# Guarded turns on a shared port in a planner, and a shorter float64 conversion: attention, experts and a feed-forward layer on one core

## The chip, the cores and the metric

The kernel runs on one core of one Trainium2 chip. The metric is the device time of one execution in microseconds (us); lower is better. The engines are TensorE (PE; its weight loads are PEld), VectorE (DVE), ScalarE (ACT), GpSimd (POOL) and SyncE (SP, which issues all DMAs here).

## The reference, cut to what matters

Three layers follow each other. Windowed attention over 4 x 576 tokens with 8 heads gives x of 2304 x 512. A mixture of eight dense experts follows, whose gate P is normalized eight times over rows and columns. The last layer is

```python
h = x @ w_in
g = np.maximum(0.01 * h, h)
return (g @ w_out).astype(np.float32)
```

with w_in of 512 x 2048 and w_out of 2048 x 512. These two arrive as **float64**, because they were scaled by a float64 factor; all else is float32. The kernel sees each float64 as two 32-bit words and makes a float32 of it on the chip, once, before the last layer needs it.

## The kernel before

**Matrix work.** Every weight and activation is split into two float16 parts, and each product is a sum of three float16 matmuls. On top of that, each pair of blocks goes through a seven-product scheme (`PRODUCTS`) in place of eight. A chunk is 512 columns of one expert (16 chunks) or of the last layer (4). For each chunk and each of five token pairs p, `a_steps` makes the hidden block and `b_steps` multiplies it back and adds it to the result `acc`. Each has groups of seven steps j, six matmuls to a step for 256 columns. L1089 is the matmul of an a step, L1205 of a b step.

**What the other engines do for a step.** ScalarE and VectorE empty PSUM: ScalarE copies products to `q` (L1101, L1113), VectorE adds into a held bank (L1105), and the outer, middle and sum blocks are split into float16 parts (`h<-...` at L1117, L1136, L1142, L1158). GpSimd subtracts the high part of the sums (`sums_lo`, L1161, 128x1024), which the b steps of the same block read. The product of a b step is added to `acc` by VectorE (L1218), or, for steps 1 and 3, by ScalarE and GpSimd (L1215, L1216). For the next chunk's weights, GpSimd forms sums (L964) and low parts (L804).

**The float64 pieces.** `to_single(n, place)` converts one piece of 128x512 float64 numbers in a staging buffer `raw` (two of them, raw_173 and raw_174 in the order below). There are 32 pieces, about three to a chunk, in chunks 1 to 11. Each has a load and these jobs: `exponent` (VectorE L1018 takes the exponent bits, ScalarE L1021 shifts and rebiases them), `signed` (VectorE L1024 adds the sign bit), `high` (VectorE L1029 masks the upper mantissa, ScalarE L1030 makes 1 + x of it), `low` (ScalarE L1036 scales the lower word, GpSimd L1038 adds it), `put` (GpSimd L1042 multiplies mantissa and exponent, SP stores the piece). L1018, L1024 and L1029 read and write SBUF alone.

**The planner.** The program is written out once, and then `Plan` orders it. It makes a node of each instruction (for TensorE, of each run of matmuls into one bank) with an estimated cost. `deadlines` walks back from TensorE's ideal sequence and gives each node a latest end. `order` plays the program forward, event by event: on each engine it picks, of the nodes that are ready, the one with the earliest latest end. `fix` pins the resulting order on every engine, without waits of its own. VectorE nodes with no PSUM operand are marked `shared`: in the plan they can't start while a GpSimd instruction runs, and a GpSimd instruction that meets one of them is stretched. On the chip nothing but the order within each engine, and the data, enforces any of that: which of the two gets the port depends on who comes first there.

**An engine's queue is in order.** An instruction that waits holds up all that stands behind it on its engine. This is why the place of the piece's instructions among the others matters.

Of the kernel before, what the change touches and what calls it, by code (L numbers as in the profile page):

```python
# [30 lines left out]
class Plan:  # L31
# [15 lines left out]
    NEAR = 60.0  # L47

# [194 lines left out]
    def deadlines(self, products):  # L243
# [5 lines left out]
        for i in products:  # L249
            t += nodes[i]["cost"] + self.TURN.get((mode, nodes[i]["mode"]), 0)  # L250
            mode = nodes[i]["mode"]
            ends[i] = t
        latest = [ends.get(i, t + 5000) for i in range(n)]
# [21 lines left out]
    def order(self, latest):  # L275
# [12 lines left out]
        gpsimd, port, mode = (0.0, 0.0), (0.0, 0.0), "full"  # L288
        self.starts = [0.0] * n

# [11 lines left out]
        def takes(i, t):  # L302

            node = nodes[i]
            cost = node["cost"]
            if node["eng"] == "PE":
                cost += self.TURN.get((mode, node["mode"]), 0)
            elif node["shared"] and gpsimd[0] <= t < gpsimd[1]:
                cost = max(cost, gpsimd[1] - t + cost - node["shared"])
            elif node["eng"] == "Pool" and port[0] <= t < port[1]:  # L310
                cost += max(0.0, port[1] - t - 140)
            return cost

        for _ in range(n):
            choices = []
            for e, w in waiting.items():
                when = [(x, i) for x, i in ((since(i), i) for i in w) if x is not None]
                if when:
                    choices.append((max(free[e], min(when)[0]), e, when))
            t, eng, when = min(choices)  # L320
            at = dict((i, x) for x, i in when)
# [4 lines left out]
            if eng != "PE" and eng != "SP":  # L326

                for i in sorted((i for i in at if i != pick and at[i] < start + cost), key=lambda i: latest[i]):
                    s = max(at[i], t)
                    c = takes(i, s)  # L330
                    if (latest[i] < latest[pick] and max(at[i], start + cost) + nodes[i]["cost"] > latest[i]
                            and s + c + nodes[pick]["cost"] <= latest[pick]):
                        pick, start, cost = i, s, c
                        break
                if nodes[pick]["shared"] and cost > nodes[pick]["cost"] + 100:
                    other = [i for i in at if i != pick and not nodes[i]["shared"] and at[i] <= start + 100
                             and max(t, at[i]) + nodes[i]["cost"] + cost <= max(latest[pick], start + cost + 200)]
# [6 lines left out]
            if eng == "PE":  # L344
                mode = node["mode"]
            elif node["shared"]:
                port = (max(start, gpsimd[1]) if gpsimd[0] <= start < gpsimd[1] else start), end
            elif eng == "Pool":
                gpsimd = start, end
            self.starts[pick] = start  # L350
# [17 lines left out]

    def fix(self):
        follows = mybir.DependencyInfo(mybir.DependencyClass.NoSync, mybir.DependencyReason.DATA)  # L370
        products = [i for i, node in enumerate(self.nodes) if node["eng"] == "PE"]
        for picks in self.order(self.deadlines(products)).values():
            line = [ins for i in picks for ins in self.nodes[i]["ins"]]
            for a, b in zip(line, line[1:]):
                self.tc.add_manual_dep(b, a.name, follows, reason="order")


@with_exitstack
def attn_moe_kernel(
# [65 lines left out]
    nc.vector.memset(shift, float(-(896 << 23)))  # L445
# [550 lines left out]
    def to_single(n, place):  # L996
# [20 lines left out]
        def exponent():  # L1017
            nc.vector.tensor_scalar(out=d["fac"], in0=d["hi"], scalar1=20, scalar2=0x7FF,  # L1018
                                    op0=ALU.logical_shift_right, op1=ALU.bitwise_and)

            nc.scalar.activation(out=d["fac"], in_=d["fac"], func=AF.Relu, scale=float(2**23), bias=shift)  # L1021

# [4 lines left out]
        def high():  # L1027

            nc.vector.tensor_scalar(out=d["man"], in0=d["hi"], scalar1=0xFFFFF, scalar2=None, op0=ALU.bitwise_and)  # L1029
            nc.scalar.activation(out=d["man"].bitcast(F32), in_=d["man"], func=AF.Relu, scale=2.0**-20,  # L1030
                                 bias=ones[:, 0:1])

        def low():

            rest = d["rest"] = words_f32(d["lo"])
            nc.scalar.activation(out=rest, in_=d["lo"].bitcast(U32), func=AF.Copy, scale=2.0**-52)  # L1036
            man = d["man"].bitcast(F32)
            nc.gpsimd.tensor_tensor(out=man, in0=man, in1=rest, op=ALU.add)  # L1038
# [6 lines left out]
        def words_f32(w):  # L1045
            return w.bitcast(F32)

        return load, [exponent, signed, high, low, put]


# [443 lines left out]
```

## Time and profile before

| | |
|---|---|
| median of 3 runs | 1856.25 us (1854.02 to 1857.41) |
| the profiled execution | 1853.38 us, span of the trace 1851.6 us |
| TensorE granted clock, mean | 0.996 |
| TensorE busy | 1812.1 us |
| VectorE, ScalarE, GpSimd busy | 1367.5, 1348.8, 1323.0 us |
| DMA | 97.81 MB, mean 53 GB/s |

The attention stage takes about the first 200 us of the trace; after that the chunks follow each other, some 83.5 us each. Busy time counts an instruction from its start to its end, so an instruction that is held at a port counts as busy. Idle time of an engine that doesn't bound the kernel costs nothing.

### The profile page before, as it was taken

How to read it: one execution, taken by the hardware profiler on the slowest of the kernel's cores; microseconds unless marked ns; L12 is line 12 of the kernel's file. 1: busy time of each engine (PE TensorE's matmuls, PEld its weight loads, DVE VectorE, ACT ScalarE, POOL GpSimd, SP SyncE). 2: the span in 40 equal slices, each digit the busy share in tenths (PEclk: the TensorE clock that was granted, in tenths of full speed). 3: DMA queues.
4: the chain of work that ended last, by engine and by line, in shares of the span. 5: the costliest groups of instructions: out<-in, count | busy, mean ns of one | idle time of the engine just before them, and what ended most of it. 6: DMA issues, size and time to landing. Idle time of an engine off the chain costs nothing.

```text
span 1851.6 us, 45040 instructions
## 1 busy us (share of the span) xinstructions
PE 1812.1 (98%) x17542; PEld 1603.7 (87%) x17542; DVE 1367.5 (74%) x3656; ACT 1348.8 (73%) x3099; POOL 1323.0 (71%) x1154
## 2 busy tenths in 40 slices
PE   8899999999999999999999999999999999999999
PEld 6677888889888888889888888889898888989888
DVE  7878677777777687777777776666676888687877
ACT  8988778767767766767767667666666789877664
POOL 3943878787869788787868777676667696776753
PEclk9999999999999999999999999999999999999999
DMA  8332020311112121202111110100000000101002
GB/s 296 109 115 76 4 81 28 87 37 62 53 47 67 32 74 37 86 27 72 53 47 53 47 52 30 47 24 24 24 24 34 15 24 24 47 1 47 1 33 72
DMA packets 61096, 97.81 MB, mean 53 GB/s; under 512 B 4561, under 2 KB 27601, under 8 KB 60881
## 3 DMA queue, kind: packets, MB, share of 16 engines
q1 hardware_dynamic: 60880, 94.93, 15.6%
q8 instruction: 137, 2.24, 0.5%
q14 instruction: 79, 0.64, 0.1%
HBM read 81.81 MB, written 13.11 MB: 51 GB/s over the span
## 4 chain that ended last, share of the span: by engine, by line
PE 76%; POOL 7%; ACT 6%; DVE 5%; DMA 4%; issue 2%; SPq 0%; POOLq 0%; DVEq 0%; ACTq 0%
PE t L1205 36%; PE s L1089 20%; PE sq L1089 15%; POOL w L804 3%; DMA raw<-in_moe_w_dram 3%; POOL h L1161 1%; PE s L570 1%; PE o L669 1%; PE pt L651 1%; ACT junk L937 1%; POOL xp L804 1%; DVE s L1117 1%; DVE raw L1018 1%; ACT raw L940 1%; DVE acc L1218 1%
## 5 line engine op out<-in xcount | busy, mean ns | idle before, releaser
L1205 PE MATMUL t<-w,h 128*128 128x256 f16 x7560 | 953.3, 273 | 7.5 <-ACT acc L1212 2.7
L1089 PEld LDWEIGHTS <-w 128*128 128x128 f16 x8400 | 757.0, 98 | 101.5 <-issue 22.9
L1205 PEld LDWEIGHTS <-h 128*128 128x128 f16 x7560 | 736.1, 98 | 97.1 <-issue 8.8
L1089 PE MATMUL s<-xp,w 128*128 128x256 f16 (+1 forms) x4872 | 591.3, 262 | 13.4 <-ACT q L1101 10.2
L1218 DVE SCALAR_TENSOR_TENSOR acc<-t,pu,acc 128x256 f32<-128x256 f32 x866 | 407.3, 479 | 173.5 <-PE t L1205 149.9
L1161 POOL TENSOR_TENSOR h<-s,h 128x1024 f16<-128x1024 f32 x180 | 386.2, 2145 | 135.1 <-ACT h L1158 95.4
L1089 PE MATMUL sq<-xp,w 128*128 128x256 f16 (+1 forms) x3528 | 429.9, 262 | 1.8 <-ACT q L1101 1.0
L1216 POOL TENSOR_TENSOR acc<-acc,part 128x256 f32<-128x256 f32 x322 | 238.9, 743 | 201.0 <-ACT part L1215 131.5
L804 POOL TENSOR_TENSOR w<-raw,w 128x512 f16<-128x512 f32 x240 | 274.7, 1162 | 28.8 <-ACT w L803 28.3
L1101 ACT ACTIVATE q<-s 128x256 f32<-128x256 f32 x364 | 138.6, 381 | 134.9 <-PE s L1089 132.3
L1158 ACT ACTIVATE h<-s 128x1024 f16<-128x1024 f32 x180 | 190.1, 1056 | 45.8 <-DVE s L1117 44.4
L1117 DVE SCALAR_TENSOR_TENSOR h<-sq,h 128x512 f16<-128x512 f32 x352 | 193.1, 553 | 34.0 <-ACT h L1136 24.4
L1215 ACT ACTIVATE part<-t,pu 128x256 f32<-128x256 f32 x322 | 152.1, 472 | 79.8 <-PE t L1205 75.0
L1105 DVE SCALAR_TENSOR_TENSOR sq<-s,q 128x256 f32<-128x256 f32 x176 | 75.8, 431 | 143.5 <-PE s L1089 86.3
L1105 DVE SCALAR_TENSOR_TENSOR sq<-sq,q 128x256 f32<-128x256 f32 x352 | 150.3, 427 | 38.1 <-PE sq L1089 33.6
L803 ACT ACTIVATE w<-raw 128x512 f16<-128x512 f32 x240 | 147.5, 631 | 12.1 <-PE s L1089 4.3
L1117 DVE SCALAR_TENSOR_TENSOR s<-sq,s 128x256 f32<-128x256 f32 x352 | 146.4, 416 | 0.7
L1136 ACT ACTIVATE h<-sq 128x512 f16<-128x512 f32 x176 | 104.9, 596 | 55.6 <-DVE sq L1105 46.5
L1117 DVE SCALAR_TENSOR_TENSOR s<-sq,q 128x256 f32<-128x256 f32 x352 | 137.1, 417 | 9.4 <-ACT q L1113 7.8
L940 ACT ACTIVATE raw<-raw,sr 128x512 f32<-128x512 f32 x160 | 109.7, 720 | 7.4 <-DVE sr L795 7.4
L937 ACT ACTIVATE junk<-raw 128x512 bf16<-128x512 f32 x160 | 100.4, 627 | 14.6 <-DMA raw<-in_moe_w_dram 9.1
L964 POOL TENSOR_TENSOR raw<-raw 128x512 f32<-128x512 f32 x80 | 102.4, 1280 | 0.0
(151 smaller groups left out, 1682.9 us busy)
## 6 DMA issues: line engine op xcount, KB each, us to landing
raw<-in_moe_w_dram SPq DMA_DIRECT2D x32, 768.0 KB, 4.7
k_t<-in_k_dram SPq DMA_DIRECT2D x16, 512.0 KB, 4.6
raw<-in_moe_w_dram SPq DMA_DIRECT2D x32, 256.0 KB, 3.6
raw<-in_moe_w_in_dram SPq DMA_DIRECT2D x16, 512.0 KB, 3.5
raw<-in_moe_w_out_dram SPq DMA_DIRECT2D x16, 512.0 KB, 3.5
q_t<-in_q_dram SPq DMA_DIRECT2D x18, 256.0 KB, 2.9
acc<-in_v_dram SPq DMA_DIRECT2D x18, 256.0 KB, 6.1
v_t<-in_v_dram SPq DMA_DIRECT2D x18, 256.0 KB, 2.7
```

The source lines that it names most:

```text
L803: nc.scalar.activation(out=hi, in_=src, func=AF.Copy)
L804: return nc.gpsimd.tensor_tensor(out=lo, in0=src, in1=hi, op=ALU.subtract)
L1089: nc.tensor.matmul(d[b][:, f, :], t[:, wp, kk, ft * P:(ft + 1) * P], XP[p][:, o, kk, xp, :], start=(i == 0 and f == 0 and j in FIRST), sto ...
L1101: nc.scalar.activation(out=q[:, k], in_=ps, func=AF.Copy, scale=CS)
L1105: nc.vector.scalar_tensor_tensor(out=block(k), in0=ps, scalar=CS, in1=q[:, k], op0=ALU.mult, op1=ALU.add)
L1117: nc.vector.scalar_tensor_tensor(out=out, in0=in0, scalar=sc, in1=in1, op0=op0, op1=op)
L1158: nc.scalar.activation(out=h[:, 3:7, 0, :], in_=d["s"], func=AF.Copy)
L1161: nc.gpsimd.tensor_tensor(out=h[:, 3:7, 1, :], in0=d["s"], in1=h[:, 3:7, 0, :], op=ALU.subtract)
L1205: nc.tensor.matmul(ps, h[:, o, hp, f, tt * P:(tt + 1) * P], w[:, wp, ft, :], start=(i == 0 and j in FIRST), stop=(i == 5), skip_group_chec ...
L1215: nc.scalar.activation(out=part, in_=ps, func=AF.Copy, scale=s)
L1216: nc.gpsimd.tensor_tensor(out=dst, in0=dst, in1=part, op=ALU.add)
L1218: nc.vector.scalar_tensor_tensor(out=dst, in0=ps, scalar=s, in1=dst, op0=ALU.mult, op1=ALU.add)
```

## The change

**In the planner.** (1) A GpSimd instruction that follows a shared VectorE instruction in the plan (`holder`) starts there only after it, and where its start falls within GUARD = 1500 ns of the holder's, the pair goes into `turns`; `fix` then gives the GpSimd instruction a real wait (a synchronizing dependency) on that VectorE instruction. The changed program has 120 such turns: 54 of them wait for a piece's VectorE instructions, most others for `dg` at line 780. (2) `claim` lets a shared VectorE instruction of over 230 ns that would start within REACH = 400 ns go ahead of the next GpSimd instruction, if neither becomes late by it. (3) A shared VectorE instruction that would meet a running GpSimd instruction is put behind its end, if its deadline allows, so that VectorE takes other work in between. (4) `lag`, the lateness of TensorE's plan so far, is added to the deadlines in those tests.

**In the pieces.** The mask gets a second bit operation that sets bit 20, so `man` holds 2^20 + the upper 20 mantissa bits as an integer. One VectorE instruction then adds the lower word times 2^-32 and writes float32. The exponent's bias is lowered by 20 to match. ScalarE's two instructions (L1030, L1036) and GpSimd's addition (L1038) go. The ScalarE job of `exponent` becomes a job of its own (`power`). Per piece, VectorE has four instructions instead of three, ScalarE one instead of three, GpSimd one instead of two. Line numbers of the changed kernel: L1018 becomes L1057, L1021 L1062, L1029 L1066, L1024 L1070, the new addition is L1075, L1042 L1080, L1161 L1196, L1216 L1251, L1218 L1253, L964 L1003, L804 L843, L1105 L1140, L1117 L1152.

```diff
+    REACH = 400.0
+    GUARD = 1500.0
...
             elif node["shared"] and gpsimd[0] <= t < gpsimd[1]:
                 cost = max(cost, gpsimd[1] - t + cost - node["shared"])
-            elif node["eng"] == "Pool" and port[0] <= t < port[1]:
-                cost += max(0.0, port[1] - t - 140)
...
+                if e == "DVE" and gpsimd[1] > free[e]:
+                    when = [(max(x, gpsimd[1]) if nodes[i]["shared"] and gpsimd[0] <= max(x, free[e]) < gpsimd[1]
+                             and latest[i] + lag > gpsimd[1] + nodes[i]["cost"] else x, i) for x, i in when]
...
+            if eng == "Pool":
+                if holder is not None:
+                    t = max(t, port[1] + self.TO["Pool"])
+                first = min((i for _, i in when if since(i) <= t + self.NEAR), key=lambda i: (latest[i], i), default=None)
+                wanted = self.claim(choices, latest, lag, free["DVE"], t, first)
+                if wanted is not None:
+                    eng, when = "DVE", [wanted]
+                    t = max(free["DVE"], wanted[0])
...
             if eng == "PE":
                 mode = node["mode"]
+                lag = max(lag, end - self.ends[pick])
             elif node["shared"]:
                 port = (max(start, gpsimd[1]) if gpsimd[0] <= start < gpsimd[1] else start), end
+                holder = pick
             elif eng == "Pool":
                 gpsimd = start, end
+                if holder is not None and start < port[0] + self.GUARD:
+                    self.turns.append((pick, holder))
+                holder = None
...
+    def claim(self, choices, latest, lag, free, t, first):
+
+        for _, e, when in choices:
+            if e == "DVE":
+                for x, i in sorted(when, key=lambda w: latest[w[1]]):
+                    a = self.nodes[i]
+                    start = max(free, x)
+                    if a["shared"] and a["cost"] > 230 and start <= t + self.REACH:
+                        late = start + a["cost"]
+                        if any(k != i and max(y, late) + self.nodes[k]["cost"] > latest[k] + lag and latest[k] < latest[i]
+                               and y <= late for y, k in when):
+                            return None
+                        if first is not None and latest[first] < latest[i] and late + self.nodes[first]["cost"] > latest[first] + lag:
+                            return None
+                        return x, i
+        return None
...
+        after = mybir.DependencyInfo(mybir.DependencyClass.Sync, mybir.DependencyReason.DATA)
+        for i, k in self.turns:
+            self.tc.add_manual_dep(self.nodes[i]["ins"][0], self.nodes[k]["ins"][-1].name, after, reason="port")
...
-    nc.vector.memset(shift, float(-(896 << 23)))
+    nc.vector.memset(shift, float(-(916 << 23)))
...
+        def mantissa():
+
+            nc.vector.tensor_scalar(out=d["man"], in0=d["hi"], scalar1=0xFFFFF, scalar2=0x100000,
+                                    op0=ALU.bitwise_and, op1=ALU.bitwise_or)
...
-        def high():
-
-            nc.vector.tensor_scalar(out=d["man"], in0=d["hi"], scalar1=0xFFFFF, scalar2=None, op0=ALU.bitwise_and)
-            nc.scalar.activation(out=d["man"].bitcast(F32), in_=d["man"], func=AF.Relu, scale=2.0**-20,
-                                 bias=ones[:, 0:1])
-
         def low():
 
-            rest = d["rest"] = words_f32(d["lo"])
-            nc.scalar.activation(out=rest, in_=d["lo"].bitcast(U32), func=AF.Copy, scale=2.0**-52)
-            man = d["man"].bitcast(F32)
-            nc.gpsimd.tensor_tensor(out=man, in0=man, in1=rest, op=ALU.add)
+            nc.vector.scalar_tensor_tensor(out=d["man"].bitcast(F32), in0=d["lo"].bitcast(U32), scalar=2.0**-32,
+                                           in1=d["man"], op0=ALU.mult, op1=ALU.add)
...
-        return load, [exponent, signed, high, low, put]
+        return load, [exponent, power, mantissa, signed, low, put]
```

**VectorE at the 28th piece** (raw_173, the first of its chunk; in the trace of before its L1018 starts at 989.63 us). sq, s and h are the PSUM banks and blocks of an a step, acc the result of a b step. Before:

```order
L1117 SCALAR_TENSOR_TENSOR s<-sq,s 128x256
L1218 SCALAR_TENSOR_TENSOR acc_107<-t_15228,pu,acc_107 128x256
L1218 SCALAR_TENSOR_TENSOR acc_109<-t_15172,pu,acc_109 128x256
L1218 SCALAR_TENSOR_TENSOR acc_110<-t_15275,pu,acc_110 128x256
L1018 TENSOR_SCALAR raw_173<-raw_173 128x512
L1105 SCALAR_TENSOR_TENSOR sq<-sq,q 128x256
L1218 SCALAR_TENSOR_TENSOR acc_109<-t_15172,pu,acc_109 128x256
L1024 SCALAR_TENSOR_TENSOR raw_173<-raw_173,sign 128x512
L1029 TENSOR_SCALAR raw_173<-raw_173 128x512
L1105 SCALAR_TENSOR_TENSOR sq<-s_15267,q 128x256
```

And now:

```order
L1152 SCALAR_TENSOR_TENSOR h<-sq,h 128x256
L1057 TENSOR_SCALAR raw_173<-raw_173 128x512
L1066 TENSOR_SCALAR raw_173<-raw_173 128x512
L1152 SCALAR_TENSOR_TENSOR s<-sq,q 128x256
L1253 SCALAR_TENSOR_TENSOR acc_109<-t_15118,pu,acc_109 128x256
L1152 SCALAR_TENSOR_TENSOR s<-sq,q 128x256
L1152 SCALAR_TENSOR_TENSOR s<-sq,s 128x256
L1253 SCALAR_TENSOR_TENSOR acc_107<-t_15174,pu,acc_107 128x256
L1152 SCALAR_TENSOR_TENSOR s<-sq,s 128x256
L1253 SCALAR_TENSOR_TENSOR acc_110<-t_15221,pu,acc_110 128x256
L1070 SCALAR_TENSOR_TENSOR raw_173<-raw_173,sign 128x512
L1075 SCALAR_TENSOR_TENSOR raw_173<-raw_173 128x512
```

The piece's instructions moved ahead of the four s sums and stand in two pairs, the exponent with the mask, and the sign with the new addition.

**GpSimd at the same place.** h is the low part of an a block's sums, w the low part of a weight. Before:

```order
L804 TENSOR_TENSOR w_15187<-raw_173,w_15187 128x512
L1216 TENSOR_TENSOR acc_107<-acc_107,part 128x256
L964 TENSOR_TENSOR t_15044<-raw_174 128x512
L1161 TENSOR_TENSOR h<-s,h 128x4x256
L964 TENSOR_TENSOR raw_174<-raw_174,t_15044 128x2x256
L1216 TENSOR_TENSOR acc_110<-acc_110,part 128x256
```

And now, with the engines that each instruction waits for (a number behind a name is the semaphore's own):

```order
L1251 TENSOR_TENSOR acc_107<-acc_107,part 128x256 [waits DVE_49]
L843 TENSOR_TENSOR w_15133<-raw_173,w_15133 128x512 [waits Activation_49]
L1196 TENSOR_TENSOR h<-s,h 128x4x256 [waits DVE_49]
L1196 TENSOR_TENSOR h<-s,h 128x4x256 [waits DVE_49,Activation_49]
L1003 TENSOR_TENSOR raw_174<-raw_174 128x2x256 [waits Pool_49]
L1251 TENSOR_TENSOR acc_110<-acc_110,part 128x256 [waits Activation_49]
```

Two h subtractions now stand in a row behind the w's; the first waits for L1066 (the mask), the second for L1075 (the addition). Before, six instructions stood between the two.

**GpSimd in the attention stage**, near 80 us of the trace. Before:

```order
L804 TENSOR_TENSOR w_732<-raw_174,w_732 128x512
L804 TENSOR_TENSOR w_735<-raw_174,w_735 128x512
L618 TENSOR_TENSOR pieces<-pieces 128x8 x2
L1161 TENSOR_TENSOR h<-s,h 128x4x256
L804 TENSOR_TENSOR w_738<-raw_174,w_738 128x512
L804 TENSOR_TENSOR w_741<-raw_174,w_741 128x512
L1161 TENSOR_TENSOR h<-s,h 128x4x256
L538 MEMSET dist 64x192
```

And now:

```order
L657 TENSOR_TENSOR pieces<-pieces 128x8 x2
L843 TENSOR_TENSOR w_729<-t_681,w_729 128x512
L1196 TENSOR_TENSOR h<-s,h 128x4x256 x2
L843 TENSOR_TENSOR w_732<-raw_174,w_732 128x512
L843 TENSOR_TENSOR w_735<-raw_174,w_735 128x512
L843 TENSOR_TENSOR w_738<-raw_174,w_738 128x512
L843 TENSOR_TENSOR w_741<-raw_174,w_741 128x512
L894 TENSOR_TENSOR sx<-acc_104 128x256
```

Both h subtractions moved ahead of four w's.

## Rows read from the trace of the kernel before

**Rows 1.** part 1 of the page: busy us, share, instructions by engine.
```profile
PE 1812.1 (98%) x17542; PEld 1603.7 (87%) x17542; DVE 1367.5 (74%) x3656; ACT 1348.8 (73%) x3099; POOL 1323.0 (71%) x1154
```

**Rows 2.** TensorE's waits, 900 to 1100 us: waiter <- releaser: total us, times, longest.
```profile
PE s L1089 <- ACT q L1101: 7.0, 3, 2.6
PE s L1089 <- DVE k L792: 0.5, 1, 0.5
```

**Rows 3.** TensorE's waits, 250 to 900 us, two of three.
```profile
PE s L1089 <- DVE sq L1105: 1.7, 6, 0.7
PE t L1205 <- DVE acc L1218: 0.7, 2, 0.5
```

**Rows 4.** TensorE's waits, 0 to 250 us, three of 17.
```profile
PE s L1089 <- ACT q L1101: 2.6, 2, 1.4
PE t L1205 <- ACT acc L1212: 1.8, 1, 1.8
PE t L1205 <- POOL h L1161: 1.6, 1, 1.6
```

**Rows 5.** timeline of the second stall: start us, us, engine, line, op, [idle before <-releaser].
```profile
989.63 3.97 DVE L1018 TENSOR_SCALAR raw<-raw 128x512 int32<-128x512 int32 x1
993.52 0.42 DVE L1105 SCALAR_TENSOR_TENSOR sq<-sq,q 128x256 f32<-128x256 f32 x1
...
988.73 1.28 POOL L964 TENSOR_TENSOR t<-raw 128x512 f32<-128x512 f32 x1
989.96 2.14 POOL L1161 TENSOR_TENSOR h<-s,h 128x1024 f16<-128x1024 f32 x1
992.05 1.27 POOL L964 TENSOR_TENSOR raw<-raw,t 128x512 f32<-128x512 f32 x1
...
993.63 0.72 ACT L1021 ACTIVATE raw<-raw,shift 128x512 int32<-128x512 int32 x1 [4.04 <-DVE raw L1018]
994.26 0.36 ACT L1101 ACTIVATE q<-s 128x256 f32<-128x256 f32 x1
...
994.68 0.82 PE L1089 MATMUL s<-xp,w 128*128 128x256 f16 x6 [2.21 <-ACT q L1101]
995.33 1.18 PE L1089 MATMUL sq<-xp,w 128*128 128x256 f16 x6
...
999.62 0.82 PE L1089 MATMUL s<-xp,w 128*128 128x256 f16 x6
```

**Rows 6.** groups by line and shape, whole run: xcount | busy us, mean ns | idle.
```profile
L1018 DVE TENSOR_SCALAR raw<-raw 128x512 int32<-128x512 int32 x32 | 31.8, 995 | 4.0 <-DMA raw<-in_moe_w_in_dram 2.4 <-DMA raw<-in_moe_w_out_dram 1.3
L1029 DVE TENSOR_SCALAR raw<-raw 128x512 int32<-128x512 int32 x32 | 23.4, 730 | 0.0
L1030 ACT ACTIVATE raw<-raw,ones 128x512 f32<-128x512 int32 x32 | 23.0, 719 | 14.7 <-DVE raw L1029 14.7
L1036 ACT ACTIVATE raw<-raw 128x512 f32<-128x512 uint32 x32 | 21.6, 675 | 0.0
L1038 POOL TENSOR_TENSOR raw<-raw 128x512 f32<-128x512 f32 x32 | 41.3, 1290 | 36.9 <-ACT raw L1036 17.6 <-DVE acc L1218 7.4 <-issue 5.7
```

**Rows 7.** instructions of a line: durations ns min/median/max, first and last start.
```profile
L1024 DVE SCALAR_TENSOR_TENSOR raw<-raw,sign x32: 741/752/1750, 236.5 to 1101.9; 128x512 int32<-128x512 int32 x32
L1018 DVE TENSOR_SCALAR raw<-raw x32: 414/650/4328, 234.1 to 1100.7; 128x512 int32<-128x512 int32 x32
```

**Rows 8.** two stretches: length, busy us (count) of each engine, granted clock, DMA.
```profile
84.20:91.20 7.00, 5.44 (x29) 3.69 (x28) 5.13 (x8) 4.81 (x16) 4.94 (x6) 0.51 0.47 152
995.60:999.10 3.50, 3.50 (x20) 2.51 (x18) 1.88 (x4) 1.87 (x4) 2.35 (x3) 0.51 0.00 0
```

**Rows 9.** timeline of a wait in the attention stage, columns as in group 5.
```profile
82.96 4.53 DVE L1117 SCALAR_TENSOR_TENSOR h<-q,h 128x768 f16<-128x768 f32 x2
...
83.84 2.83 POOL L1161 TENSOR_TENSOR h<-s,h 128x1024 f16<-128x1024 f32 x1
...
86.73 2.96 PE L1205 MATMUL t<-w,h 128*128 128x256 f16 x13 [1.56 <-POOL h L1161]
```

More of the change, by code (lines that the diff above doesn't have):

```diff
@@ L252, in deadlines @@
             ends[i] = t
+        self.ends = ends
         latest = [ends.get(i, t + 5000) for i in range(n)]
@@ L287, in order @@
         closed = dict.fromkeys(self.users, 0.0)
-        gpsimd, port, mode = (0.0, 0.0), (0.0, 0.0), "full"
+        gpsimd, port, mode, holder = (0.0, 0.0), (0.0, 0.0), "full", None
         self.starts = [0.0] * n
+        self.turns = []
+        lag = 0.0
         def since(i):
@@ L330, in order @@
                     c = takes(i, s)
-                    if (latest[i] < latest[pick] and max(at[i], start + cost) + nodes[i]["cost"] > latest[i]
-                            and s + c + nodes[pick]["cost"] <= latest[pick]):
+                    if (latest[i] < latest[pick] and max(at[i], start + cost) + nodes[i]["cost"] > latest[i] + lag
+                            and s + c + nodes[pick]["cost"] <= latest[pick] + lag):
                         pick, start, cost = i, s, c
@@ L336, in order @@
                     other = [i for i in at if i != pick and not nodes[i]["shared"] and at[i] <= start + 100
-                             and max(t, at[i]) + nodes[i]["cost"] + cost <= max(latest[pick], start + cost + 200)]
+                             and max(t, at[i]) + nodes[i]["cost"] + cost <= max(latest[pick] + lag, start + cost + 200)]
                     if other:
@@ L1019, in exponent, with power @@
                                     op0=ALU.logical_shift_right, op1=ALU.bitwise_and)
+        def power():
             nc.scalar.activation(out=d["fac"], in_=d["fac"], func=AF.Relu, scale=float(2**23), bias=shift)
+        def mantissa():
+            nc.vector.tensor_scalar(out=d["man"], in0=d["hi"], scalar1=0xFFFFF, scalar2=0x100000,
+                                    op0=ALU.bitwise_and, op1=ALU.bitwise_or)
         def signed():
@@ L1043, in put @@
             nc.sync.dma_start(dst, man)
-        def words_f32(w):
-            return w.bitcast(F32)
-        return load, [exponent, signed, high, low, put]
+        return load, [exponent, power, mantissa, signed, low, put]
     Ht = {}
```

## The prediction

> **What bounds the kernel now.** I read the page's busy times first: TensorE is busy 1812.1 of 1851.6 us, VectorE, ScalarE and GpSimd 71 to 74% [rows 1]. So work that is taken off those three is worth nothing in itself; only TensorE's idle time, some 39 us, and stretches at half its clock can be won. Next I read TensorE's waits by stage. From 900 to 1100 us there are three equal ones, 7.0 us together, on ScalarE's copy q [rows 2]. From 250 to 900 us the listed waits come to little, 1.7 us in six on VectorE's sq and 0.7 us in two on acc [rows 3]. Before 250 us, in the attention stage, they are many and of many kinds; three are shown [rows 4].
>
> The timeline of the second stall names the cause [rows 5]. VectorE's exponent instruction L1018 starts at 989.63 and lasts 3.97 us, though L1018 takes 0.41 us at its shortest [rows 7]. In that time GpSimd runs three instructions back to back, 988.73 to 993.32 us, two of which began after L1018 had. L1018 ends 0.28 us behind the third. ScalarE's L1021 waits 4.04 us for it, and L1101, whose copy TensorE needs, stands behind L1021 in ScalarE's queue. TensorE loses 2.21 us. Then its granted clock falls to 0.51, the 1.2 GHz level, from about 995.6 on [rows 8]. From 995.33 to 999.62 us it does four groups of six matmuls in 4.29 us [rows 5]; at full speed a group starts 0.65 us behind the last (994.68 to 995.33), so the four cost 1.67 us more.
>
> The Trainium skill, page "SBUF — State Buffer", section "Who interferes with whom", says of the port pair that VectorE and GpSimd share that whichever "starts first gets the pair for the whole instruction; the other fully blocks". The trace agrees that one blocks the other, but not on who gets it next: by the rule L1018 would have gone when L964 ended at 990.01, and would have been done by 990.43; it ended at 993.60. By the rule no such stall exists for a guard to remove; by the row each costs about 2.3 us.
>
> **The change part by part**, against the profiled execution of 1853.38 us.
>
> *Guard and order at the three stalls.* The three are the first pieces of their chunks. In the new order the GpSimd subtraction that could overtake L1057 (the old L1018) waits for L1066 behind it, so at most one GpSimd instruction, already running, is still ahead of the pair. By the order excerpt that is a w of a weight or a shorter sum into acc. Chunks that didn't stall in this way still lost about 0.2 us once each (the six waits of 1.7 us, less the longest of 0.7, leave five of 0.2 [rows 3]). I take 7.0 down to 0.6: **-6.4 us**; bounds 0 (if the wait is only moved) and -7.0.
>
> *The clock behind the second stall.* It fell only there, after a 2.21 us stop; with no stop I take back the 1.67: **-1.7**; bounds 0 and -1.7.
>
> *Blocked VectorE work, 250 to 900 us.* L1018 averages 0.995 us and L1029, of the same shape, 0.730, against 0.414 for the shortest L1018; L1024 takes up to 1.75 against a median of 0.75 [rows 6, 7]. The waits there sum to 2.4 us [rows 3]; I take a third: **-0.8**; bounds 0 and -2.4.
>
> *What the pieces lose and gain in work.* ScalarE loses 32 x 0.719 + 32 x 0.675 = 44.6 us, GpSimd 32 x 1.290 = 41.3 us [rows 6]. Both lie beside TensorE, which had no wait on any of the three lines: **0**. Were that cover gone, they would be a gain only. VectorE gains L1075. No row shows it; the nearest is L1024, also two SBUF inputs of 512, 0.75 us at the median; bounds 0.41 (one input, L1018) and 1.75 (L1024 when held). So 32 x 0.75 = 24.0 us is added. The old three came to at least 0.995 + 0.75 + 0.730 = 2.48 us a piece (L1024 at its median); four that aren't held are 2 x 0.41 + 2 x 0.75 = 2.32. VectorE's sum thus hardly changes, and its 26% idle time hides it: **0**. If it weren't hidden, a pair of 1.5 us in the queue ahead of L1140 (the old L1105) would stop ScalarE and TensorE as L1018 did; that is the third rival.
>
> *The guards' own cost.* The 120 waits hold GpSimd, and behind it its queue: acc sums, sums and low parts of weights, the h subtractions. GpSimd has 29% idle, so most are hidden; h is the one that TensorE reads soon. A late h has cost TensorE 1.56 us once [rows 9]. No row shows a guard; bounds 0 and nine times 1.56 = 14, since nine chunks have an h behind each of the two pairs. I take half a microsecond in total for GpSimd's smaller delays, and 0.3 for shifts of order in the late chunks: **+0.8**.
>
> *The attention stage.* At 82.96 us VectorE's two h subtractions take 4.53 us, held by GpSimd; GpSimd's h, itself held (2.83 us against 2.14 at 989.96 [rows 5]), ends at 86.67, and TensorE has waited 1.56 for it [rows 9]. The clock is then at 0.51 over 84.2 to 91.2 us [rows 8]. The new order puts both GpSimd h ahead of four w's, which should end this wait; but in this stage one engine's relief is soon another's wait (2.6 us on q, 1.8 on acc [rows 4], neither at the port), and the whole order of the stage is made anew. I take the 1.56 alone: **-1.5**; bounds -8.7 (the wait; half of TensorE's 5.44 busy us in the slow stretch, 2.7; and the 2.6 and 1.8 of the other waits) and +4.3 (another wait like it, with its slow stretch).
>
> Sum: -6.4 - 1.7 - 0.8 + 0.8 - 1.5 = **-9.6 us**, so 1843.8 for an execution like the profiled one. That one was 2.87 us below the median of 1856.25, against which runs are compared; I give the time on that footing: 1856.25 - 9.6 = 1846.65, rounded to **1846.5 us**.
>
> **The rivals.**
>
> *The first of each pair still waits its turn (13%).* The guard acts on the GpSimd instruction after the pair, not on the one before. If the one ahead is an h, L1057 waits up to 2.14 us, and pair and wait take 2.14 + 2 x 0.41 = 2.96 instead of 3.97. Each stall shrinks by 1.0 us only, -3.0, and with the -0.8 of the blocked work it comes to about 1852.5. For it: VectorE has no guard against GpSimd. Against: the order excerpt has no h directly ahead.
>
> *The page's rule decides (2%).* If a held VectorE instruction always went next, the three stalls would have another cause and the guards would only make GpSimd wait: the -6.4 and -1.7 go, the time is 1856.25 - 1.5 = 1854.8. The page is the Trainium skill's "SBUF — State Buffer", cited above. Rows 5 speak against it.
>
> *The guard makes h late (10%, the slower side).* The second h of a pair waits for L1075, which stands in VectorE's queue behind sums into acc that wait for TensorE. TensorE then waits for GpSimd for VectorE for TensorE. At 1.56 us in nine chunks that is +14.0, and with the sum above 1856.25 - 9.6 + 14.0 = 1860.7. It decides from 9.6 / 9 = 1.07 us in each chunk. For it: the excerpt shows both h's in a row, later in GpSimd's queue than before. Against: over the whole run TensorE waited for an h only once [rows 4].
>
> *The attention stage falls into place (15%).* If the wait at 85 us and the low clock behind it both go, and the 1.8 on acc too, the stage gives 1.56 + 2.7 + 1.8 = 6.1 instead of 1.5: about 1842. For it: VectorE held by GpSimd stands at the root of the first two. Against: q and acc wait for ScalarE, which the change relieves only after this stage.
>
> That the guard doesn't exist as a wait is excluded: the order excerpt shows the semaphore of VectorE on both h.
>
> **How the numbers follow.** The forecast has 60%, and its own range from the bounds of the clock, the small waits and the attention stage is about 1841 to 1852. The rivals have 13, 2, 10 and 15%. A measurement here tells some 0.2%, 3.7 us, from no change: below 1852.5 is faster, above 1860 slower. Faster: nearly all of 60 (58), 15, and half of 13 (6): 79%. Slower: 6 of the 10 of the late h, whose price is just above the bound, and 2 for an attention stage that got worse: 8%. Same: the rest, 13%. Eight times in 10 it lies between 1839 and 1856: the low end is the lucky attention stage with the small waits gone, the high end the rule of the page and a little more.
>
> **What would show it.** The longest L1057 is below 2.6 us instead of 4.33; TensorE's waits between 900 and 1100 us come to about 1 us instead of 7.5, with full clock there; L1030, L1036 and L1038 have no successor, and busy time falls by about 45 us on ScalarE and 41 on GpSimd, with the span only 10 us shorter. The forecast is wrong if TensorE's waits name L1196 (the late h), if L1057 still shows 4 us, or if the first 250 us lose or win more than 5.

## The result, and the profile after

The changed kernel took **1837.85 us** in the median of 4 runs (1836.86 to 1843.13), the kernel before 1856.83 in the same comparison (1854.02 to 1868.97). The ratio is 0.9891 with an interval of 0.9844 to 0.9939: 1.1% faster, about twice the 9.6 us forecast, and 1.15 us below the range. The profiled execution of after took 1843.13 us (span 1841.3), the slowest of its four. A second profile of the same kernel (1839.62 us, span 1837.9, experiment 5) is read beside it.

Part 1 of the page, as [rows 1]:

```profile
PE 1808.0 (98%) x17542; PEld 1603.2 (87%) x17542; DVE 1331.9 (72%) x3688; ACT 1317.1 (72%) x3035; POOL 1267.4 (69%) x1122
```

VectorE has 32 instructions more and yet is busy for 35.6 us less, where the prediction had it hardly changed; ScalarE fell by 31.7 us and GpSimd by 55.6, where it had about 45 and 41. TensorE's waits from 900 to 1100 us [rows 2] are gone: the view lists none there, nor anywhere from 860 to 1130 us. From 250 to 860 us, where [rows 3] were (waiter <- releaser: total us, times, longest):

```profile
PE t L1240 <- DVE acc L1253: 2.0, 6, 0.6
PE sq L1124 <- ACT q L1136: 1.9, 2, 1.6
PE s L1124 <- DVE k L828: 0.9, 2, 0.5
PE t L1240 <- ACT part L1250: 0.6, 1, 0.6
```

And from 0 to 250 us, as [rows 4]. The 1.6 us on an h has become 0.3; the acc is later than before (2.9 us against 1.8), and the 2.6 us on rb lies at 17 us, ahead of any piece:

```profile
PE pt L690 <- ACT rb L680: 3.3, 2, 2.6
PE t L1240 <- ACT acc L1247: 2.9, 1, 2.9
...
PE s L1124 <- ACT q L1136: 1.6, 2, 1.2
...
PE rt L664 <- POOL h L1196: 0.3, 1, 0.3
```

The timeline of the 28th piece, whose L1018 stood for 3.97 us in [rows 5] (start us, us, engine, line, op, [idle before <- releaser]):

```profile
984.13 0.42 DVE L1057 TENSOR_SCALAR raw<-raw 128x512 int32<-128x512 int32 x1
...
984.46 0.42 DVE L1066 TENSOR_SCALAR raw<-raw 128x512 int32<-128x512 int32 x1
984.58 0.72 ACT L1062 ACTIVATE raw<-raw,shift 128x512 int32<-128x512 int32 x1 [0.59 <-DVE raw L1057]
...
984.96 2.13 POOL L1196 TENSOR_TENSOR h<-s,h 128x1024 f16<-128x1024 f32 x1 [0.91 <-DVE raw L1066]
...
985.57 0.38 ACT L1136 ACTIVATE q<-s 128x256 f32<-128x256 f32 x1 [0.27 <-PE s L1124]
...
987.30 0.74 DVE L1070 SCALAR_TENSOR_TENSOR raw<-raw,sign 128x512 int32<-128x512 int32 x1
...
987.96 0.69 DVE L1075 SCALAR_TENSOR_TENSOR raw<-raw 128x512 f32<-128x512 uint32 x1
...
988.79 2.13 POOL L1196 TENSOR_TENSOR h<-s,h 128x1024 f16<-128x1024 f32 x1 [1.70 <-DVE raw L1075]
```

Now GpSimd waits and VectorE does not. The first h stands 0.91 us for L1066, the second 1.70 us for L1075, and ScalarE gets to q (L1136) at once. No VectorE instruction of a piece is held by more than 0.4 us any more, at this place or elsewhere; the instructions of a line (durations ns min/median/max), as [rows 7]:

```profile
L1057 DVE TENSOR_SCALAR raw<-raw x32: 415/426/616, 233.7 to 1091.2; 128x512 int32<-128x512 int32 x32
L1066 DVE TENSOR_SCALAR raw<-raw x32: 415/420/424, 234.2 to 1091.6; 128x512 int32<-128x512 int32 x32
L1070 DVE SCALAR_TENSOR_TENSOR raw<-raw,sign x32: 740/743/1135, 235.2 to 1092.6; 128x512 int32<-128x512 int32 x32
L1075 DVE SCALAR_TENSOR_TENSOR raw<-raw x32: 678/684/689, 235.9 to 1093.3; 128x512 f32<-128x512 uint32 x32
```

GpSimd pays, as its groups show (count | busy us, mean ns | idle before, with the releasers):

```profile
L1196 POOL TENSOR_TENSOR h<-s,h 128x1024 f16<-128x1024 f32 x180 | 383.9, 2133 | 151.2 <-ACT h L1193 73.6 <-DVE acc L1253 21.7 <-DVE raw L1075 15.1
L1251 POOL TENSOR_TENSOR acc<-acc,part 128x256 f32<-128x256 f32 x322 | 232.9, 729 | 175.1 <-ACT part L1250 62.7 <-DVE raw L1075 28.6 <-DVE dg L819 19.5
L1080 POOL TENSOR_TENSOR raw<-raw 128x512 f32<-128x512 f32 x32 | 40.8, 1275 | 55.3 <-DVE raw L1075 54.1 <-DVE k L828 1.2
```

Some 98 us of waits on L1075 lie in GpSimd's idle time. Of these, 54 us stand before L1080, which multiplies what L1075 wrote and would wait for it without a guard. The guards account for the other 44 us, for 27 us on L1066 and for some 20 on dg. The listed waits of TensorE name GpSimd for 0.3 us in all. In the attention stage, the place of [rows 9] now reads:

```profile
85.28 2.14 POOL L1196 TENSOR_TENSOR h<-s,h 128x1024 f16<-128x1024 f32 x1 [0.42 <-DVE s L1152]
...
87.43 0.22 PE L664 MATMUL rt<-identb,pieces 128*112 128x128 bf16 x1 [0.29 <-POOL h L1196]
...
87.49 0.71 PE L1240 MATMUL t<-w,h 128*128 128x256 f16 x5
```

The h is no longer held (2.14 us against 2.83) and TensorE passes it with 0.29 us lost. The clock, as [rows 8] (window: length, busy us (count) of PE, PEld, DVE, ACT, POOL, granted clock, DMA):

```profile
20.90:27.90 7.00, 6.39 (x41) 4.65 (x39) 3.61 (x18) 5.72 (x21) 0.00 (x0) 0.51 0.85 295
84.20:91.20 7.00, 6.61 (x102) 5.34 (x100) 6.49 (x16) 6.67 (x18) 5.62 (x4) 1.00 0.14 40
184.70:188.30 3.60, 3.32 (x17) 2.32 (x17) 0.92 (x2) 2.51 (x7) 3.60 (x4) 0.53 0.00 0
975.00:1000.00 25.00, 25.00 (x232) 22.41 (x229) 17.36 (x42) 16.76 (x35) 22.39 (x20) 1.00 0.06 22
```

The stretches of before at 84 and 996 us are at 2.4 GHz now. One at 185 us is still there, as before (186.6 to 190.2 us at 0.53), and one at 21 us, which before's profiled execution did not have. In the second profile of after neither is there; its clock is 1.00 throughout:

```profile
16.00:28.00 12.00, 9.85 (x96) 7.17 (x96) 8.81 (x40) 10.62 (x38) 0.39 (x1) 1.00 1.04 366
...
180.00:190.00 10.00, 8.16 (x122) 7.46 (x122) 2.83 (x7) 8.44 (x20) 10.00 (x9) 1.00 0.01 2
```

**Where the time went.** All kernels have the same 17542 matmuls, so the start of the n-th in one trace can be set against the n-th in before's. The table gives how much of this difference arises in each stretch of before's time, in us (- is time won):

| kernel | 0–76 | 76–94 | 94–212 | 212–860 | 860–1119 | 1119–1840 | all |
|---|---|---|---|---|---|---|---|
| after | +4.7 | -5.2 | -1.2 | +2.4 | -10.6 | -0.4 | -10.3 |
| after, second profile | +1.6 | -5.2 | -2.7 | +3.2 | -10.6 | 0.0 | -13.8 |
| 1, new planner alone | +1.3 | -5.2 | -2.7 | -1.4 | -8.9 | -0.5 | -17.5 |
| 2, new pieces alone | +2.7 | 0.0 | 0.0 | +1.9 | -4.6 | -1.2 | -1.3 |
| 3, without the waits | +3.8 | -0.9 | -0.9 | +15.9 | -5.1 | +1.2 | +13.9 |
| 4, waits alone | +2.0 | +0.6 | 0.0 | 0.0 | -8.4 | +1.9 | -3.9 |
| 6, without the lag | +4.9 | -4.5 | +0.1 | +2.0 | -8.6 | -3.2 | -9.2 |
| 7, pieces' waits alone | +4.7 | -2.5 | -2.6 | +3.6 | -10.4 | +1.0 | -6.1 |
| 8, without the claim | +4.7 | -2.4 | -1.1 | +13.7 | -3.7 | +1.0 | +12.2 |
| 9, before once more | +3.0 | -0.3 | -1.5 | +2.2 | -5.5 | -1.0 | -3.0 |
| 10, a wait for every turn | +3.1 | -5.2 | -2.7 | +2.3 | -10.5 | +0.2 | -12.8 |
| 11, planner alone again | +4.4 | -5.2 | -1.1 | -0.7 | -8.8 | +0.2 | -11.3 |

The first column is mostly the low clock at 20 us and what follows from it; before's profiled execution was lucky there. Row 9 is the measure of chance between two executions of one kernel: 5.5 of the 10.6 us at 860 to 1119 us went there with no change at all, since two of the three stalls did not come.

### The profile page after: what moved, and what is told of

It reads as the page before. It is cut to its first block, busy times and chain, and to the rows that moved or that the text cites. A ratio compares the mean times of both kernels' runs of the same rounds, so it can differ in the third digit from the quotient of the medians.

```text
span 1841.3 us, 44982 instructions
## 1 busy us (share of the span) xinstructions
PE 1808.0 (98%) x17542; PEld 1603.2 (87%) x17542; DVE 1331.9 (72%) x3688; ACT 1317.1 (72%) x3035; POOL 1267.4 (69%) x1122
## 4 chain that ended last, share of the span: by engine, by line
PE 79%; POOL 5%; DMA 5%; DVE 5%; ACT 5%; issue 2%; SPq 0%; DVEq 0%; POOLq 0%; ACTq 0%
PE t L1240 37%; PE s L1124 21%; PE sq L1124 15%; DMA raw<-in_moe_w_dram 2%; POOL w L843 2%; DMA raw<-in_moe_w_in_dram 2%; PE s L609 2%; PE o L708 1%; PE pt L690 1%; POOL h L1196 1%; DVE s L1152 1%; ACT junk L976 1%; DVE acc L1253 1%; POOL acc L1251 1%; ACT raw L979 1%
## 5 line engine op out<-in xcount | busy, mean ns | idle before, releaser
L1253 DVE SCALAR_TENSOR_TENSOR acc<-t,pu,acc 128x256 f32<-128x256 f32 x866 | 405.5, 479 | 154.5 <-PE t L1240 124.0
L1196 POOL TENSOR_TENSOR h<-s,h 128x1024 f16<-128x1024 f32 x180 | 383.9, 2133 | 151.2 <-ACT h L1193 73.6
L1251 POOL TENSOR_TENSOR acc<-acc,part 128x256 f32<-128x256 f32 x322 | 232.9, 729 | 175.1 <-ACT part L1250 62.7
L843 POOL TENSOR_TENSOR w<-raw,w 128x512 f16<-128x512 f32 x240 | 274.7, 1162 | 64.5 <-ACT w L842 64.3
L1136 ACT ACTIVATE q<-s 128x256 f32<-128x256 f32 x364 | 138.9, 382 | 118.0 <-PE s L1124 112.6
L1152 DVE SCALAR_TENSOR_TENSOR h<-sq,h 128x512 f16<-128x512 f32 x352 | 192.4, 552 | 29.1 <-ACT h L1171 20.9
L1140 DVE SCALAR_TENSOR_TENSOR sq<-s,q 128x256 f32<-128x256 f32 x176 | 75.9, 431 | 172.2 <-PE s L1124 117.0
L1140 DVE SCALAR_TENSOR_TENSOR sq<-sq,q 128x256 f32<-128x256 f32 x352 | 150.1, 427 | 35.1 <-PE sq L1124 31.1
L1152 DVE SCALAR_TENSOR_TENSOR s<-sq,q 128x256 f32<-128x256 f32 x352 | 137.8, 417 | 20.6 <-ACT q L1148 19.7
L1152 DVE SCALAR_TENSOR_TENSOR s<-sq,s 128x256 f32<-128x256 f32 x352 | 146.2, 415 | 0.6
L1003 POOL TENSOR_TENSOR raw<-raw 128x512 f32<-128x512 f32 x80 | 101.9, 1273 | 0.0
```

The lines of the kernel that those rows point to most:

```text
L843: return nc.gpsimd.tensor_tensor(out=lo, in0=src, in1=hi, op=ALU.subtract)
L1136: nc.scalar.activation(out=q[:, k], in_=ps, func=AF.Copy, scale=CS)
L1140: nc.vector.scalar_tensor_tensor(out=block(k), in0=ps, scalar=CS, in1=q[:, k], op0=ALU.mult, op1=ALU.add)
L1152: nc.vector.scalar_tensor_tensor(out=out, in0=in0, scalar=sc, in1=in1, op0=op0, op1=op)
L1196: nc.gpsimd.tensor_tensor(out=h[:, 3:7, 1, :], in0=d["s"], in1=h[:, 3:7, 0, :], op=ALU.subtract)
L1251: nc.gpsimd.tensor_tensor(out=dst, in0=dst, in1=part, op=ALU.add)
```

## The experiments

Beside experiments 1 to 4 the kernel before had a median of 1854.41 us (23 runs), beside 5 to 8 of 1860.46 (17), beside 9 to 11 of 1858.08 (13). Ratios are against these.

**1. The new planner with the old pieces**, so that only the order and its waits are new.

```diff
...
-        return load, [exponent, power, mantissa, signed, low, put]
+        return load, [exponent, signed, high, low, put]
```

> The new planner with its guards, and the float64 pieces as they were. Theory (the three stalls of 900 to 1100 us are VectorE passed over at the port, and the guard ends them; the shorter pieces take work off engines that don't bound): about all of the gain is here, 1838 to 1842 us, the longest exponent instruction of a piece under 2.6 us, TensorE's waits of 900 to 1100 us under 1.5 us. Rival (the gain comes from the work that the pieces no longer do, since ScalarE's copies and GpSimd's sums come sooner): 1850 us or more.

Measured: 1837.11 us (1834.33 to 1840.46), ratio 0.9907 (0.9888 to 0.9927), 0.9 us below the theory's range. The planner brings the whole gain. The pieces' VectorE instructions are held now and then, L1057 by 1.1 us at most:

```profile
L1057 DVE TENSOR_SCALAR raw<-raw x32: 414/427/1519, 229.4 to 1083.9; 128x512 int32<-128x512 int32 x32
```

**2. The new pieces with the old planner.**

```diff
...
-        return load, [exponent, signed, high, low, put]
+        return load, [exponent, power, mantissa, signed, low, put]
```

> The new float64 pieces with the old planner, no guard. Theory: nothing protects VectorE at the port, so stalls of 2 us in some chunks stay and the attention stage is that of before: 1848 to 1857 us, with at least one piece's exponent instruction over 3 us. Rival (the work removed is what pays): 1842 us or less, with no such stall.

Measured: 1850.27 us, ratio 0.9980 (0.9969 to 0.9992), no more than the kernel before differs from itself (experiment 9). With ScalarE and GpSimd relieved, one of the three long stalls of L1018 still came, at 1074 us, as in experiment 9:

```profile
L1018 DVE TENSOR_SCALAR raw<-raw x32: 416/485/4296, 236.7 to 1100.3; 128x512 int32<-128x512 int32 x32
```

**3. The new order without the 120 waits**: `order` is as in after, `fix` adds no synchronizing dependency.

```diff
...
-        for i, k in self.turns:
-            self.tc.add_manual_dep(self.nodes[i]["ins"][0], self.nodes[k]["ins"][-1].name, after, reason="port")
```

> The changed kernel without the 120 waits: the same order on every engine, but no GpSimd instruction waits for VectorE at the port. Theory (the wait itself keeps GpSimd from overtaking): the VectorE instructions of the pieces are passed over again, some take over 3 us, and 4 to 10 us of the gain go: 1842 to 1850 us. Rival (the order alone, which keeps port users apart, does it; the waits are idle): within 2 us of the changed kernel's 1838, longest exponent instruction under 2.6 us.

Measured: 1865.35 us, ratio 1.0061 (1.0042 to 1.0080), slower than before, and 15 us above the theory's range, though no instruction of a piece took the 3 us that it named. Without the wait GpSimd starts early, VectorE is held by it in most chunks (L1054 is after's L1057, L1072 its L1075), and the sums into acc come late:

```profile
L1054 DVE TENSOR_SCALAR raw<-raw x32: 414/662/2490, 237.5 to 1113.3; 128x512 int32<-128x512 int32 x32
L1072 DVE SCALAR_TENSOR_TENSOR raw<-raw x32: 674/682/2614, 241.1 to 1115.8; 128x512 f32<-128x512 uint32 x32
```

TensorE's waits from 250 to 860 us:

```profile
PE t L1237 <- DVE acc L1250: 7.4, 7, 1.3
PE s L1121 <- ACT q L1133: 2.9, 6, 1.3
PE sq L1121 <- ACT q L1133: 2.6, 2, 1.8
```

The table has the loss where the pieces lie: +15.9 us from 212 to 860 us. By itself the new order costs time.

**4. The waits alone**: before with `holder`, `turns` and the loop of experiment 3, everything else in before's order.

```diff
             elif eng == "Pool":
                 gpsimd = start, end
+                if holder is not None and start < port[0] + self.GUARD:
+                    self.turns.append((pick, holder))
+                holder = None
```

> The kernel before, in its old order on every engine, with the waits alone: each GpSimd instruction that follows a shared VectorE instruction within 1500 ns of the plan waits for it. Theory: the 4 us exponent instructions of the three chunks shrink to under 2.6 us and the 7.0 us of waits with the 1.7 us of low clock mostly go: 1846 to 1850 us, the attention stage as before. Rival (a wait put into an order that wasn't made for it only makes GpSimd late): TensorE waits for h or for sums into acc, 1855 us or more.

Measured: 1850.16 us, ratio 0.9970 (0.9956 to 0.9984). The stalls of 860 to 1119 us mostly go (-8.4 in the table, of which chance alone made 5.5 in row 9), but the attention stage keeps its wait, which is longer than the 1.6 us of [rows 4]. The gain of 0.3% is little more than the 0.2% by which before differed from itself. From 0 to 250 us:

```profile
PE t L1214 <- POOL h L1170: 3.0, 1, 3.0
```

**5. The changed kernel once more**, unchanged, for a second profile.

> The changed kernel once more, to see an execution whose first 30 us are not slowed. The profiled execution of the change lost 4.7 us on before's within its first 60 us (a wait of 2.58 us at 17 us and 6.8 us at half clock behind it). Theory (that loss comes and goes with the start of an execution and belongs to neither kernel): the median stays at 1836 to 1839 us, and in a profile without it TensorE is 6 to 7 us ahead of before at 212 us and about 17 us ahead at the end. Rival (the new order causes it): every execution has it, and the profile shows it again.

Measured: 1839.76 us (1839.03 to 1843.84), ratio 0.9889 (0.9862 to 0.9915). The profile is the one quoted above. It has no low clock at 20 us, so the new order doesn't force it; TensorE is 6.3 us ahead of before at 212 us, but 13.8 and not 17 at the end.

**6. Without the lag**: the planner no longer lets deadlines slip by what TensorE is behind.

```diff
                 mode = node["mode"]
-                lag = max(lag, end - self.ends[pick])
```

> The changed kernel with lag held at 0, so that deadlines are TensorE's ideal ones, as in the planner before. Theory (guard and order do the work, lag only spares needless swaps): 1836 to 1842 us. Rival (lag is what lets a VectorE instruction wait for the port's end, since against ideal deadlines everything is late after the attention stage): VectorE is held again, 1845 us or more.

Measured: 1841.26 us, ratio 0.9891 (0.9865 to 0.9916), as after. VectorE is held again at single places, and it costs nothing that can be measured:

```profile
L1065 DVE TENSOR_SCALAR raw<-raw x32: 410/420/2243, 237.1 to 1097.2; 128x512 int32<-128x512 int32 x32
```

**7. Only the pieces' 54 waits.**

```diff
-                if holder is not None and start < port[0] + self.GUARD:
+                if holder is not None and start < port[0] + self.GUARD and nodes[holder]["writes"][0][0].startswith("raw"):
```

> The changed kernel, same order on every engine, but only the 54 waits on a piece's VectorE instructions are kept; the 66 on dg, on sums and on h are dropped. Theory (the waits serve each stage where they stand): the 900 to 1100 us stalls stay away, but the 5.7 us that the change wins near 85 us go, as those guards are gone: 1842 to 1847 us. Rival (in the attention stage the order alone does it): 1836 to 1839 us.

Measured: 1848.73 us, ratio 0.9934 (0.9910 to 0.9958). This is 1.7 us above the theory's range. The stalls stay away (-10.4), but half of the gain at 76 to 94 us is lost. No dg lies in that stretch. In after, the w of L843 waits there for two sums s (L1152) on VectorE:

```profile
82.47 0.75 DVE L1152 SCALAR_TENSOR_TENSOR s<-q 128x256 f32<-128x256 f32 x2
...
83.70 1.16 POOL L843 TENSOR_TENSOR w<-t,w 128x512 f16<-128x512 f32 x1 [1.14 <-DVE s L1152]
```

Here the w goes ahead, the two sums take 3.31 us in place of 0.75, and TensorE stands 1.84 us for pb (L695), which VectorE copies after them:

```profile
82.37 1.87 POOL L843 TENSOR_TENSOR w<-t,w 128x512 f16<-128x512 f32 x1
...
83.48 3.31 DVE L1152 SCALAR_TENSOR_TENSOR s<-q 128x256 f32<-128x256 f32 x2
...
89.16 0.66 PE L690 MATMUL pt<-ident,e 128*128 128x128 f32 x4 [1.84 <-DVE pb L695]
```

Elsewhere dg, which the other waits mostly guard, is held up to 2.88 us:

```profile
L819 DVE TENSOR_SCALAR dg<-identb,e x51: 204/460/2878, 16.3 to 1698.0; 128x128 bf16<-128x128 bf16 x51
```

In after its median is 247 ns. The 66 waits that have nothing to do with the pieces are worth 0.9934 - 0.9889 = 0.45%, some 8 us (9.0 between the medians of 7 and 5), and so about 4 tenths of the gain. How much of it is dg's and how much the sums' was not separated.

**8. Without the claim**: a shared VectorE instruction no longer goes ahead of the GpSimd instruction that the plan would start.

```diff
-                if wanted is not None:
+                if wanted is not None and False:
```

> The changed kernel without the claim: no VectorE instruction is put ahead of GpSimd's next one, so GpSimd is seldom told to wait and VectorE must wait for the end of a GpSimd instruction. Theory (claim is a refinement; guard and postponing carry the gain): 1838 to 1844 us. Rival (without claim the VectorE instructions of a piece find no gap, and sit behind deadlines): 1846 us or more.

Measured: 1863.88 us, ratio 1.0022 (1.0004 to 1.0039), as the rival had it: the whole gain goes. The guards have little to hold when the order puts GpSimd first; GpSimd's listed waits on a piece's VectorE instructions, those of L1080 left out, come to 17.5 us against 70 in after. The timeline at the first piece of a chunk:

```profile
319.82 1.27 POOL L1003 TENSOR_TENSOR raw<-raw,t 128x512 f32<-128x512 f32 x1
...
320.95 4.41 DVE L1057 TENSOR_SCALAR raw<-raw 128x512 int32<-128x512 int32 x1
...
321.05 2.12 POOL L1196 TENSOR_TENSOR h<-s,h 128x1024 f16<-128x1024 f32 x1
...
323.14 0.72 POOL L1251 TENSOR_TENSOR acc<-acc,part 128x256 f32<-128x256 f32 x1
...
323.82 1.26 POOL L1003 TENSOR_TENSOR raw<-raw 128x512 f32<-128x512 f32 x1
...
325.46 0.72 ACT L1062 ACTIVATE raw<-raw,shift 128x512 int32<-128x512 int32 x1 [2.57 <-DVE raw L1057]
325.62 0.42 DVE L1140 SCALAR_TENSOR_TENSOR sq<-s,q 128x256 f32<-128x256 f32 x1
...
326.09 0.81 PE L1124 MATMUL s<-xp,w 128*128 128x256 f16 x6 [1.66 <-DVE sq L1140]
```

It is the stall of [rows 5] again, by one instruction longer: when L1057 begins, the L1003 of 319.82 us is running, and three more GpSimd instructions that began after L1057 pass it. From 250 to 860 us TensorE waits 13.1 us on sq, in seven waits.

**9. The kernel before once more.**

> The kernel before, profiled once more. The span of every profile so far is TensorE's idle time, plus half of its time at 1.2 GHz, plus some 1808 us; the profiled execution of before had 13.7 us at 1.2 GHz. Theory (the change's larger part is low clock that typical executions of before have and those of the change don't): a slower execution of before differs from the first by low clock, not by waits: idle time again 36 us within 3, and 14 to 22 us at 1.2 GHz. Rival (it is waits that differ between executions): idle time over 40 us.

Measured: 1854.79 us in 10 runs against 1858.08 in 13 of the same kernel, ratio 0.9979 (0.9961 to 0.9998). Such a difference is what chance makes here, and ratios nearer to 1 are not told from it. The profiled execution was the shortest of the ten (1850.36 us), so it can't show what the longest lose: inconclusive for that. It does show that the stalls come by luck. Of three only the last came, at 1074 us (L1018 for 4.31 us). At the first, where L1018 had stood for 3.96 us in the profile before (from 903.05 on), it now got its turn when the GpSimd instruction ahead was done, and the h behind was held instead:

```profile
905.52 1.29 POOL L964 TENSOR_TENSOR t<-raw 128x512 f32<-128x512 f32 x1
...
906.46 0.65 DVE L1018 TENSOR_SCALAR raw<-raw 128x512 int32<-128x512 int32 x1
...
906.76 2.34 POOL L1161 TENSOR_TENSOR h<-s,h 128x1024 f16<-128x1024 f32 x1
```

**10. A wait for every turn** (GUARD = 1.0e9), and **11. the planner alone once more**, side by side.

```diff
-    GUARD = 1500.0
+    GUARD = 1.0e9
```

> The changed kernel with GUARD so large that each GpSimd instruction that follows a shared VectorE instruction in the plan waits for it, however late it is planned; same order. Theory (GpSimd instructions planned later than 1500 ns after the port's user come later on the chip too, so the added waits are idle): as the changed kernel, 1836 to 1841 us. Rival (some of the VectorE instructions at 1.1 to 1.6 us that the change still has are overtaken by unguarded ones): 1834 us or less.

> The new planner with the old pieces again, now beside the full change with all guards on the same chip. Theory (work taken off ScalarE and GpSimd is worth nothing on its own): the two within 3 us of each other. Rival (with the port ordered, the shorter pieces do pay): this one over 3 us slower.

Measured: 1839.88 us, ratio 0.9898 (0.9866 to 0.9931), and 1838.23 us, ratio 0.9893 (0.9863 to 0.9923). More waits bring nothing more, and 1.65 us between old and new pieces can't be told from none.

## Why the prediction was wrong in size

The mechanism was right: the guard and the order remove VectorE's long stands at the port, and experiments 1, 3, 4 and 8 show that order, claim and waits are all needed for it. The forecast was too small by 1846.5 - 1837.85 = 8.65 us. Against the profiled execution of before (1853.38) the sum was 1843.8; the second profile of after took 1839.62, close to the median of 1839.76 that it belongs to. So 4.2 us are the terms', 2.9 us the footing, and 1.8 lie between this profile and the other median of the same kernel (1837.85); 0.15 of rounding goes off. By the second profile, term by term:

- **The attention stage, -1.5, was the step that failed most.** Up to 212 us it gave 1.6 - 5.2 - 2.7 = -6.3, so the prediction's own sign of being wrong (more than 5 us won in the first 250) came; of the -2.7, chance alone made 1.5 in row 9. Every profile with the whole new planner has the -5.2 between 76 and 94 us. It is near the price that the prediction gave to the rival "falls into place" (6.1): the 1.56 us wait and the low clock behind it went together, and the sum took back the wait alone. That rival's third part, the wait on acc, did not go but grew from 1.8 to 2.9 us. Nor has the sum a term for what the 66 waits outside the pieces bring: without them the median was 9.0 us longer (experiment 7), and half of the 5.2 went, at a place where the wait is for sums s.
- **The three stalls with the clock, -6.4 and -1.7**, gave -10.6 from 860 to 1119 us: right in kind, 2.5 too small against a profile of before that happened to have all three. No wait is listed there any more, where 0.6 had been left over, nor the 0.5 on k of [rows 2].
- **The clock, -1.7**, is better read over the whole span. The profile of before has three stretches at half clock, 6.8 us at 84, 3.4 at 187 and 3.4 at 996 us, and the second profile of after none: half of 13.6 is 6.8 us. TensorE's busy time fell by 7.1 us, from 1812.1 to 1805.0, and its idle time (span less busy) by 6.65, from 39.5 to 32.9; the two make up the 13.8. Without its clock the forecast had 9.6 - 1.7 = 7.9, so the idle time was about right and the clock mis-sized fourfold. The second profile is a lucky one in this: the first still has 10.2 us at half clock. But the median clocks of many executions, 0.995 of before and 0.999 of after, say the same, some 7 us (0.4% of 1850, an estimate).
- **Blocked VectorE, -0.8**, was wrong in sign: +3.2 from 212 to 860 us. Profiles with the new pieces, the claim and waits have +2.0 to +3.6 there, the two with the old pieces and the new planner -1.4 and -0.7; but before's own second profile has +2.2. After's waits there are on acc, q and k, and L1070 and L1075 stand in VectorE's queue ahead of sums into acc. In the three profiles with the new pieces and all of the planner and its waits (after twice, experiment 10), TensorE's listed waits on VectorE's acc come to 1.7 to 2.6 us from 250 to 860 us; in the two with the old pieces to 0.2 us and to none. That L1070 and L1075 cause them is argued, not shown, and the times of experiments 10 and 11 don't separate it. "VectorE's work: 0" is thus unproven by up to some 4 us.
- **The guards' own cost, +0.8**, was about nothing as far as the trace shows it: TensorE's only listed wait for GpSimd is 0.3 us.
- **Work taken off ScalarE and GpSimd at 0** was right: experiment 2 has their relief and a ratio of 0.998.
- **The footing.** I carried over the 2.87 us by which the profiled execution was better than the median, as if they belonged to any kernel. They belong to before. Its 63 executions in the experiments have a median clock of 0.995; they take 1864.8 us on average at 0.993 (5 of them), 1854.1 at 0.996 (16) and 1851.6 at 0.999 (2). The ten of after have a median clock of 0.999. That stalls which come by luck make this spread is argued, not shown: both profiles of before, with three stalls (1853.38 us) and with one (1850.36), lie below its median, and no profile shows a slow execution.
- **Two readings of before were off.** The listed waits from 250 to 900 us come to 3.0 us and not 2.4, for the third line (0.6 on q) was left out. And the semaphore of VectorE on both h shows no guard by itself, since an h also reads s, which VectorE writes; the trace of after shows the guard, as 0.91 us for L1066.

Of the rivals, the first of a pair that still waits (L1057 at most 0.62 us), the late h (0.3 us) and the page's rule fell. The Trainium skill, page "SBUF — State Buffer", section "Who interferes with whom", has the later engine fully blocked for the whole of the holder's instruction (the words that the prediction quotes stand in the same page's section "SBUF: two separate sides"). That agrees with experiment 9 at 906 us, where L1018 went next. At 320.95 us in experiment 8, L1057 stayed blocked beyond that: three more GpSimd instructions passed it.

## What to carry to other kernels

When two engines share a port and the trace shows one of them passed over by several instructions of the other, put the sensitive one first in the order and hold the other by a real wait: here the order without the wait cost 0.6%, the wait without the order brought 0.3%, and both together 1.1%. Look for every instruction that is held there and not only for those behind the stalls that one profile shows: 4 tenths of the gain came from waits outside the pieces. Price a stop of TensorE together with the low clock that follows it in the trace, in every stage and not only where the change aims. The distance of the profiled execution to the median belongs to the kernel that was profiled; here the changed kernel did not keep it.

## What was not expected of the hardware

- Who gets the port next is not fixed, and who came first does not decide it alone: the same L1018 of the same kernel took 3.96 us in one execution and 0.65 us in another (experiment 9). In both it began some 0.4 us before the GpSimd instruction ahead ended (0.37 and 0.35).
- A stop of TensorE is followed by the low clock in one execution and not in the next. In after, a stop of 2.93 us from 182.0 us on led into 3.4 us at half clock from 184.8 on; the second profile has a stop of 2.94 us at 178.9, and the clock stays at 1.00. Six profiles have this stop, and in three of them the low clock follows. All thirteen profiles have a stop on rb at 17 to 18 us: ten, with stops of 1.52 to 2.58 us, show the low clock behind it, three, with 1.33 to 1.48 us, don't. No run varied that stop alone, so what decides it stays open.
- L1075, a multiplication and an addition on two 32-bit integer inputs with a float32 result, took 0.68 us at the median, against 0.74 for L1070, which has inputs of the same size and an integer result.
